# Keys laid out in SBUF as the queries are, and one transfer for each tile of four heads

## Chip, cores and metric

The kernel runs on one core of a Trainium2 chip. The metric is the device time of one execution in microseconds; the median of three runs of the kernel before is 1680.61. An interval or a verdict, where one stands, is against runs of that kernel on the same chip.

## What is computed

Packed attention, and on its output two feed-forward layers, the second gated. There are 8 batches of 8 heads, 576 tokens of 64 numbers each; 32 packing queries `p` per head stand between. All inputs and outputs are in HBM, the weights as float64, everything else as float32.

```
def sm_attn(qq, kk, vv):
    s = scale * np.matmul(qq, kk.transpose(0, 1, 3, 2))
    s = s - np.max(s, axis=-1, keepdims=True)
    a = np.exp(s)
    a = a / (np.sum(a, axis=-1, keepdims=True) + 1e-09)
    return np.matmul(a, vv)
p_packed = sm_attn(p, k, v)
out = sm_attn(q, p_packed, p_packed)
...
h = x @ w_in;  g = h * (1.0 / (1.0 + np.exp(-1.702 * h)));  x = g @ w_out
...
out = (silu(x @ w_gate) * (x @ w_val)) @ w_out2
```

The first softmax runs over the 576 keys of a head, so the order of the keys may be any, if the probabilities meet the values `v` in the same order. The values lie in chunks of 128 neighbouring tokens on the partitions.

## The kernel before, in words

PE computes in a form of three passes: each float32 operand is split into a rounded part and a rest (`split`, L205: a copy on ACT, a subtraction on DVE or POOL), and `mm3` (L215) multiplies three pairs of the parts.

Attention goes batch by batch, and in a batch by two groups `g` of four heads (HG = 4), whose 4 x 32 rows fill the 128 partitions. A batch has four raw tiles of 128 x 18 x 64 (576 KB): keys of group 0 and 1 (`load_raw` with j = 0, 1, L260) and queries of group 0 and 1 (j = 2, 3, L263). There are 8 x 4 = 32 such tiles; each comes by four DMAs on SP's queue, one per head. Of a key tile, partition i of a head holds tokens 64n + 2i and 64n + 2i + 1 for n from 0 to 8, so that the runs in HBM are 512 B. Of a query tile, partition i holds the tokens 18i to 18i + 17, one run of 4608 B. The raw tiles have three buffers, which in the first batch weights and a split query share.

`do_T` (L347) transposes a raw tile in 32 x 32 blocks on DVE, once for each half of the 64 numbers; `split_T` (L355) splits the result; `sc1` (L358) multiplies the packing queries with 320 and then 256 columns of keys into PSUM; `max1` (L367) takes the maximum; `exp1` (L375) writes the exponentials with ACT into SBUF, and on this way puts the keys into their natural order; `norm1`, `a1T`, `copy_a1T`, `pv` divide by the sum, transpose on PE, and multiply with the values. `do_D`, `sc2`, `max2`, `exp2`, `norm2` are the second attention, and `do_z` folds its packed values into the first layer's weights, so that `p1` (L554) and `p2` (L574) compute the first layer directly from the second attention's probabilities.

In the first batch the weights come too: `stage` (L294) loads float64 tiles of 512 KB, `rebias` and `to_f32` (L188, L193) turn them into float32 on ACT and DVE, `split_w` (L490) splits w_in and stores the parts to HBM with DMAs that ACT issues (L497); `split_out` does it for w_out. Later batches load the split w_in back (`load_win`, L284). While PE has nothing else, `warm` (L241) gives it matmuls without use.

The order around the change is written out by hand: FIRST (L19) is the list of steps of the first batch and of the beginning of the second, SECOND and STEADY go beside the units of the first layer. The language's planner takes the instructions in this order as priorities and places each on its engine by its own estimates of durations, so that an engine's order can differ from the list. It also gives the DMAs of SP and ACT one of eight completion semaphores in turn, and has a DMA wait until the DMA that had its semaphore before has landed. Each engine and each queue executes in order.

The first layer ends at about 855 us. From then on the second layer works without attention.

Of the kernel before, what the change touches and what calls it, by code (L numbers as in the profile page):

```python
# [11 lines left out]
AF = mybir.ActivationFunctionType  # L12
# [97 lines left out]
def kernel(  # L110
# [27 lines left out]
    PE, ACT, DVE, POOL, SP = nc.tensor, nc.scalar, nc.vector, nc.gpsimd, nc.sync  # L138
# [7 lines left out]
    G = H * NPK // P  # L146
    HG = H // G
# [5 lines left out]
    NBLK = S // 32  # L153
    NSC = 5
    TAIL = S - 4 * P
    HK = (5 * HS // 9 * 2, S - 5 * HS // 9 * 2)
# [95 lines left out]
    def load_raw(i):  # L252
        b, j = divmod(i, 2 * G)
        if b >= B:
            return
        src, g = (k, j) if j < G else (q, j - G)
        t = at.tile([P, NBLK, D], F32, tag="raw", bufs=3, name="raw")
        for h in range(HG):
            if j < G:
                SP.dma_start(out=t[32 * h:32 * h + 32].rearrange("p (n r) d -> p n (r d)", r=2),  # L260
                             in_=src[b, g * HG + h].rearrange("(n i r) d -> i n (r d)", i=32, r=2))
            else:
                SP.dma_start(out=t[32 * h:32 * h + 32].rearrange("p n d -> p (n d)"),  # L263
                             in_=src[b, g * HG + h].rearrange("(i n) d -> i (n d)", i=32))
        raw[i] = t

    def load_v(b, g):
# [59 lines left out]
    def attention(b):  # L327
        st = {}
# [46 lines left out]
        def exp1(g):  # L375
            a = at.tile([P, S], F32, tag="a1", bufs=2, name="a1")
            s = at.tile([P, 4], F32, tag="sm1", bufs=2, name="sm1")
            for t in range(2):
                o = a[:, t * HK[0]:t * HK[0] + HK[t]].rearrange("p (n i r) -> p n r i", i=32, r=2)
                ACT.activation(o, st["sc1", g][t][:, :HK[t]].rearrange("p (n r i) -> p n r i", i=32, r=2), AF.Exp,  # L380
                               bias=st["mx1", g][:, 3:4], scale=SCALE, accum_out=s[:, t:t + 1])
            st["e1", g], st["sm1", g] = a, s

# [139 lines left out]
        def raw_ahead(n):  # L523
            load_raw(b * 2 * G + n + 3)
# [338 lines left out]
    def issue(text, ops, ops_next=None):  # L863
        for x in text.split(";"):
            f, *a = x.split()
            f = ops_next[f[1:]] if f[0] == "+" else ops[f]
            f(*[int(c) if c.isdigit() else engines.get(c, c) for c in a])

    ops = dict(attention(0), load_p=load_p, load_raw=load_raw, load_v=load_v, make_consts=make_consts, stage=stage,
               rebias=lambda *k: rebias(k), to_f32=lambda kind, j, eng=ACT: to_f32((kind, j), eng), split_out=split_out, p1=u_p1, act1=u_act1,  # L870
               warm=warm,               act2=lambda n, eng=DVE: act2(units[n], eng), p2=lambda n: p2(units[n]))
    second = attention(1)
    issue(FIRST, ops, second)
    for n in range(16 + LAG, len(units)):
        b, u = units[n][0], n % NU
# [16 lines left out]
        if b == B - 1:  # L892
# [5 lines left out]
            if u in (2, 3, 21, 22, 25, 26, 29, 30):  # L898
                j = (2, 3, 21, 22, 25, 26, 29, 30).index(u)
# [79 lines left out]
```

## Time and profile before

| | us |
|---|---|
| median of three runs | 1680.61 (1678.06 to 1680.67) |
| the profiled execution | 1680.02 |
| its span, first to last instruction | 1678.3 |
| PE busy in it | 1643.6 (98%) |
| DVE, ACT, POOL busy | 1145.3, 782.1, 287.7 |
| mean granted clock of PE | 0.996 of full speed |

A row of the timeline gives the start, the busy time, engine and line, the operation with its output and inputs, how many instructions it merges, and in brackets how long the engine stood before it and what ended that. SPq and ACTq are the queues of SP and ACT that issue DMAs. `win` are the split weights in HBM, `wh` their tiles in SBUF, `w64in` and `w64out` the float64 tiles, `raw` the keys and queries, `sc` scores, `z` the folded weights, `h` and `acc` the first layer's two products. A DMA share over 1 is a few per cent of overlap in the count of busy engines.

### The profile page before, as it was taken

What the parts mean: (1) busy time and instruction counts of PE and PEld (TensorE: products, weight loads), DVE (VectorE), ACT (ScalarE), POOL (GpSimd) and SP (SyncE); (2) the same over time, 40 slices, a digit from 0 to 9 for tenths busy, and PEclk for the clock granted to TensorE, in tenths of its full rate; (3) what the DMA queues carried; (4) which work ended last, traced back from release to release, by engine and by line L of the source; (5) the groups of instructions that cost most, each with busy time, mean ns of one, the idle gap of its engine ahead of it and who ended that gap; (6) DMA issues with size and microseconds to landing.
All of it is one profiled execution on the core that took longest, in us unless ns stands there. A gap on an engine that the chain in (4) does not pass through costs nothing.

```text
span 1678.3 us, 26277 instructions
## 1 busy us (share of the span) xinstructions
PE 1643.6 (98%) x9516; PEld 1472.7 (88%) x9516; DVE 1145.3 (68%) x2161; ACT 782.1 (47%) x1662; POOL 287.7 (17%) x240
## 2 busy tenths in 40 slices
PE   9789999999999999999999999999999999999998
PEld 8679999999999999999988888888888888888887
DVE  6877878686876868777688366666657565746562
ACT  5775756566575656656554222242224222422222
POOL 2332313131221313121122111000100010001010
PEclk9999999999999999999999999999999999999999
DMA  8965767557474755526488544435444444425411
GB/s 237 341 234 130 219 187 220 175 174 229 128 232 137 220 169 173 184 90 215 152 296 317 178 162 158 145 113 168 158 145 151 130 159 145 158 75 176 145 51 51
DMA packets 169346, 290.63 MB, mean 173 GB/s; under 512 B 54784, under 2 KB 96768, under 8 KB 169216
## 3 DMA queue, kind: packets, MB, share of 16 engines
q1 hardware_dynamic: 165760, 280.03, 52.2%
q10 hardware_dynamic: 3456, 8.91, 1.4%
q8 instruction: 75, 1.23, 0.3%
q14 instruction: 55, 0.45, 0.1%
HBM read 230.16 MB, written 58.72 MB: 172 GB/s over the span
## 4 chain that ended last, share of the span: by engine, by line
PE 83%; DVE 6%; DMA 4%; issue 3%; ACT 2%; POOL 1%; SPq 0%; ACTq 0%; POOLq 0%; DVEq 0%
PE acc L217 36%; PE gv L217 30%; PE h L217 10%; PE sc L217 3%; PE pv L412 2%; PE zp L516 2%; DMA win<-wh 2%; DVE z L519 1%; DMA wh<-win 1%; DVE gh L207 1%; DVE g L566 1%; PE a1T L395 1%; DVE T L347 0%; POOL gh L207 0%; DMA w64in<-in_moe_w_in_dram 0%
## 5 line engine op out<-in xcount | busy, mean ns | idle before, releaser
L217 PE MATMUL gv<-xh,w 128*128 128x512 f32 x2304 | 554.4, 389 | 0.0
L217 PEld LDWEIGHTS gv<-xh,w 128*128 128x128 f32 x2304 | 432.4, 188 | 89.7
L217 PE MATMUL acc<-gh,wo 128*128 128x288 f32 x3072 | 457.1, 296 | 4.6 <-ACT wo L206 2.7
L217 PEld LDWEIGHTS acc<-gh,wo 128*128 128x128 f32 x3072 | 426.8, 189 | 9.0 <-ACT wo L206 3.5
L217 PE MATMUL acc<-wo,gh 128*128 128x512 f32 x1296 | 326.8, 389 | 0.4
L217 PEld LDWEIGHTS acc<-wo,gh 128*128 128x128 f32 x1296 | 243.0, 188 | 52.0 <-DVE c L211 1.6
L217 PE MATMUL h<-a,z 128*128 128x288 f32 x1536 | 251.7, 298 | 8.6 <-DVE g L566 6.8
L207 DVE TENSOR_TENSOR gh<-g,gh 128x288 fp32r<-128x288 f32 (+1 forms) x295 | 175.8, 596 | 92.7 <-ACT gh L206 89.8
L217 PEld LDWEIGHTS h<-a,z 128*128 128x128 f32 x1536 | 222.0, 189 | 16.8 <-DVE g L566 7.9
L206 ACT CAST gh<-g 128x288 fp32r<-128x288 f32 (+1 forms) x304 | 140.1, 462 | 156.1 <-DVE g L566 108.0
L207 POOL TENSOR_TENSOR gh<-s,gh 128x512 fp32r<-128x512 f32 x60 | 82.8, 1380 | 699.5 <-ACT gh L206 655.7
L810 DVE TENSOR_TENSOR c<-gv,c 128x512 f32<-128x512 f32 x192 | 132.2, 688 | 84.2 <-ACT tb L825 56.7
L206 ACT CAST gh<-s 128x512 fp32r<-128x512 f32 x60 | 37.2, 621 | 247.0 <-DVE s L821 229.2
L566 DVE SCALAR_TENSOR_TENSOR g<-sig,h 128x288 f32<-128x288 f32 x256 | 113.9, 445 | 41.9 <-ACT sig L564 37.9
L564 ACT ACTIVATE sig<-h 128x288 f32<-128x288 f32 x256 | 104.3, 408 | 76.4 <-PE h L217 73.4
L810 DVE TENSOR_TENSOR ta<-gv,c 128x512 f32<-128x512 f32 x96 | 66.2, 689 | 83.4 <-PE gv L217 83.4
L521 POOL TENSOR_TENSOR z<-z,z 128x512 fp32r<-128x512 f32 x56 | 74.9, 1338 | 175.7 <-ACT z L520 175.7
L519 DVE TENSOR_TENSOR z<-zp,z 64x512 f32<-64x512 f32 x112 | 76.5, 683 | 15.2 <-ACT z L518 12.3
L830 ACT ACTIVATE s<-c 128x512 f32<-128x512 f32 x48 | 30.3, 632 | 96.0 <-DVE c L810 96.0
L518 ACT COPY z<-zp 64x512 f32<-64x512 f32 x112 | 65.1, 581 | 13.0 <-PE zp L516 10.8
L516 PE MATMUL zp<-wh,E 128*128 128x512 f32 x224 | 66.6, 400 | 4.6 <-DMA wh<-win 2.7
L814 ACT ACTIVATE s<-ta 128x512 f32<-128x512 f32 x48 | 30.3, 632 | 69.1 <-DVE ta L810 69.1
(134 smaller groups left out, 1574.9 us busy)
## 6 DMA issues: line engine op xcount, KB each, us to landing
w<-w2s SPq DMA_DIRECT2D x144, 512.0 KB, 3.3
wh<-win SPq DMA_DIRECT2D x112, 512.0 KB, 4.2
w2s<-w SPq DMA_DIRECT2D x36, 512.0 KB, 3.8
w<-w2s SPq DMA_DIRECT2D x48, 256.0 KB, 2.6
raw<-in_k_dram SPq DMA_DIRECT2D x64, 144.0 KB, 4.4
raw<-in_q_dram SPq DMA_DIRECT2D x64, 144.0 KB, 3.3
x2d<-x SPq DMA_DIRECT2D x16, 576.0 KB, 3.3
w2d<-f SPq DMA_DIRECT2D x36, 256.0 KB, 3.1
```

The lines of the kernel that those rows point to most:

```text
L206: ACT.copy(dst[:, 0], src)
L207: eng.tensor_tensor(out=dst[:, 1], in0=src, in1=dst[:, 0].bitcast(F32), op=ALU.subtract)
L217: PE.matmul(o, lhsT=lhs(a), rhs=rhs(c), start=first and n == 0, stop=last and n == 2)
L412: PE.matmul(ps[:, c].rearrange("p h i -> p (h i)"), lhsT=vv[:n, k, 2 * c:2 * c + 2].rearrange("p h d -> p (h d)"), rhs=st["a1T", g][:n, k, ...
L516: PE.matmul(ps, lhsT=E[:, c].rearrange("p a i -> p (a i)"), rhs=w[c][:, d], start=d == 0, stop=d == 1)
L518: ACT.copy(x[o], ps[r])
L519: DVE.tensor_tensor(out=x[o], in0=ps[o], in1=x[o], op=ALU.add)
L521: POOL.tensor_tensor(out=y[:, 1], in0=x, in1=y[:, 0].bitcast(F32), op=ALU.subtract)
L564: ACT.activation(s, ps[:, :HS], AF.Tanh, scale=0.5 * 1.702)
L566: DVE.scalar_tensor_tensor(out=g, in0=s, scalar=1.0, in1=ps[:, :HS], op0=ALU.add, op1=ALU.mult)
L810: DVE.tensor_tensor(out=o, in0=ps, in1=c, op=ALU.add)
L814: ACT.activation(s1, ta, AF.Tanh, scale=0.5)
```

## The change

The branch for keys in `load_raw` goes: keys are laid out as queries are, tokens 18i to 18i + 17 on partition i of a head. The loop over the four heads goes too: one DMA brings 128 partitions of 4608 B, which are one piece of 576 KB in HBM. The column (n, i) of a score block is now the token 18i + n, so `exp1` writes 10 and then 8 blocks of 32 with a step of 18 elements in its output, where it wrote with a step of 2. Sizes and number of all other instructions stay as they are.

```
 def load_raw(i):
...
     t = at.tile([P, NBLK, D], F32, tag="raw", bufs=3, name="raw")
-    for h in range(HG):
-        if j < G:
-            SP.dma_start(out=t[32 * h:32 * h + 32].rearrange("p (n r) d -> p n (r d)", r=2),
-                         in_=src[b, g * HG + h].rearrange("(n i r) d -> i n (r d)", i=32, r=2))
-        else:
-            SP.dma_start(out=t[32 * h:32 * h + 32].rearrange("p n d -> p (n d)"),
-                         in_=src[b, g * HG + h].rearrange("(i n) d -> i (n d)", i=32))
+    SP.dma_start(out=t.rearrange("p n d -> p (n d)"),
+                 in_=src[b, g * HG:g * HG + HG].rearrange("h (i n) d -> (h i) (n d)", i=32))
...
 def exp1(g):
...
     for t in range(2):
-        o = a[:, t * HK[0]:t * HK[0] + HK[t]].rearrange("p (n i r) -> p n r i", i=32, r=2)
-        ACT.activation(o, st["sc1", g][t][:, :HK[t]].rearrange("p (n r i) -> p n r i", i=32, r=2), AF.Exp,
+        o = a.rearrange("p (i n) -> p n i", n=NBLK)[:, t * HK[0] // 32:(t * HK[0] + HK[t]) // 32]
+        ACT.activation(o, st["sc1", g][t][:, :HK[t]].rearrange("p (n i) -> p n i", i=32), AF.Exp,
                        bias=st["mx1", g][:, 3:4], scale=SCALE, accum_out=s[:, t:t + 1])
```

## Rows read from the trace of the kernel before

**Rows 1.** Windows: length, busy PE, PEld, DVE, ACT, POOL (x count), PE clock, DMA share, GB/s.

```profile
0.00:35.00 35.00, 31.43 (x232) 29.38 (x232) 22.16 (x57) 15.90 (x33) 7.69 (x15) 1.00 0.81 216
35.00:110.00 75.00, 57.88 (x342) 49.51 (x342) 59.26 (x105) 57.01 (x119) 23.47 (x21) 0.93 0.94 319
110.00:200.00 90.00, 86.67 (x614) 82.74 (x613) 72.26 (x158) 60.41 (x142) 32.15 (x27) 1.00 0.58 170
200.00:855.00 655.00, 650.10 (x4730) 635.27 (x4729) 492.70 (x1077) 403.70 (x954) 141.57 (x118) 1.00 0.58 181
```

**Rows 2.** Waits of PE from 200 to 855 us: total, times, longest.

```profile
PE zp L516 <- DMA wh<-win: 2.3, 5, 0.6
```

**Rows 3.** Windows of shorter stretches, same columns.

```profile
3.00:5.00 2.00, 2.00 (x11) 2.00 (x11) 1.00 (x2) 0.62 (x1) 0.20 (x1) 1.00 1.03 242
20.00:35.00 15.00, 14.72 (x116) 13.50 (x115) 11.08 (x30) 6.72 (x17) 3.31 (x3) 1.00 0.70 205
40.00:50.00 10.00, 8.22 (x43) 6.27 (x44) 9.54 (x19) 7.27 (x14) 2.05 (x2) 1.00 1.02 392
100.00:105.00 5.00, 4.03 (x19) 4.03 (x20) 4.19 (x8) 4.13 (x8) 2.04 (x2) 0.66 0.67 158
```

**Rows 4.** Timeline of SP's queue to 32 us: start, length of the issues, line.

```profile
1.31 1.95 SPq L260 DMA_DIRECT2D raw<-in_k_dram  x4
...
5.77 0.93 SPq L298 DMA_DIRECT2D w64in<-in_moe_w_in_dram  x2
9.78 2.19 SPq L263 DMA_DIRECT2D raw<-in_q_dram  x4
...
18.93 0.63 SPq L298 DMA_DIRECT2D w64in<-in_moe_w_in_dram  x1
27.13 2.84 SPq L274 DMA_DIRECT2D vt<-in_v_dram  x5
```

**Rows 5.** Waits of SP's queue, up to 110 us: total, times, longest.

```profile
SPq L274 <- DMA win<-wh: 10.8, 3, 7.6
```

**Rows 6.** Tile raw, DMAs issued from 1.2 to 3.2 us.

```profile
DMA to landing us min/median/max: 2.7/2.9/3.2
```

**Rows 7.** Timeline of DVE and ACT, 6 to 12 us.

```profile
6.14 1.44 DVE L347 STREAM_TRANSPOSE T<-raw 128x576 f32<-128x576 f32 x2 [2.08 <-DMA raw<-in_k_dram]
...
9.79 0.66 ACT L190 ACTIVATE f<-w64in 128x512 f32<-128x512 f32 x1 [1.50 <-DMA w64in<-in_moe_w_in_dram]
```

**Rows 8.** Timelines of SP, ACT, DVE, PE near 95 us, and tile raw there.

```profile
91.89 6.25 SPq L260 DMA_DIRECT2D raw<-in_k_dram  x8
...
96.95 0.59 ACT L206 CAST z<-zp 128x512 fp32r<-128x512 f32 x1 [2.32 <-DMA raw<-in_k_dram]
...
98.61 0.78 DVE L347 STREAM_TRANSPOSE T<-raw 128x576 f32<-128x576 f32 x1 [3.75 <-DMA raw<-in_k_dram]
...
100.97 1.44 PE L217 MATMUL h<-a,z 128*128 128x288 f32 x6 [4.76 <-DVE g L566]
...
DMA to landing us min/median/max: 2.9/4.7/5.1
```

**Rows 9.** Groups of ACT by shape: count, busy us, mean ns, idle before.

```profile
L206 ACT CAST gh<-g 128x288 fp32r<-128x288 f32 x256 | 110.4, 432 | 109.2 <-DVE g L566 108.0
...
L206 ACT CAST gh<-g 128x512 fp32r<-128x512 f32 x48 | 29.7, 620 | 46.8 <-PE acc L217 46.8
...
L380 ACT ACTIVATE a<-sc,mx 128x320 f32<-128x320 f32 x16 | 8.8, 549 | 5.5 <-DVE mx L372 5.5
...
L380 ACT ACTIVATE a<-sc,mx 128x256 f32<-128x256 f32 x16 | 7.8, 486 | 0.0
```

**Rows 10.** Chain of the first 110 us: shares by line; start, length.

```profile
by line: DMA win<-wh 27.8%; DMA w64in<-in_moe_w_in_dram 5.9%; issue 5.6%; DMA raw<-in_q_dram 5.1%; PE pv L412 4.3%; DMA raw<-in_k_dram 4.2%; PE sc L217 3.4%; DVE wh L207 3.0%; POOL wo L207 2.9%; DVE T L347 2.5%; POOL wh L207 2.5%; DMA pt<-i
...
82.04 9.76 DMA win<-wh
```

**Rows 11.** Timeline of ACT's queue near 24 us.

```profile
24.04 0.93 ACTq L497 DMA_DIRECT2D win<-wh  x2
```

## The prediction

> **What bounds the kernel now.** I read the page's first part, then the span by stages, then PE's waits in the long middle stage, and at last the start of the kernel engine by engine. By the page PE is busy nearly all the time; the stages say where it isn't [rows 1]: in the first 110 us PE lacks 3.6 + 17.1 = 20.7 us, and some of what it does there is only the filler of `warm`; from 110 to 200 us it lacks 3.3, and in the 655 us after that 4.9. From 855 us on the kernel has no attention in it, so the change can't reach that. In the middle the change can save at most those 3.3 + 4.9 us, and the largest wait of PE in the second of them is 2.3 us for weights that come back from HBM [rows 2], not a key, a query or a softmax. So the change is decided in the first 110 us, where DMA is the fullest resource (0.81, then 0.94 of its time) and PE the one with holes.
>
> Two things are to be seen in that start. First, what a key costs. While key tile 0 alone is in flight, 3 to 5 us, the DMA engines are full (1.03) and move 242 GB/s; with 4 KB rows, 40 to 50 us, as full (1.02) they move 392 [rows 3]. Second, the queue. SP issues the 13th DMA at 9.78 us though the 12th was out at 6.70, and after 19.56 it issues nothing until 27.13 [rows 4]; it stood there for the landing of a weight store, 7.6 us [rows 5]. The program gives its DMAs eight completion semaphores in turn, those of SP and ACT together, and a DMA is not issued before the one eight places back has landed. Four small DMAs per tile eat four of the eight places.
>
> **The change, part by part.** 128 DMAs of keys and queries become 32. An issue takes 0.45 us (four in 1.95) [rows 4], so some 43 us of SP's time go, over 700 us, nearly all beside other work. Terms, with gains negative:
>
> (a) The first key. The four DMAs go out at 1.31 to 2.8, and land 2.7 to 3.2 us after each issue [rows 6], the last at 6.0; DVE waits for it 2.08 us until 6.14 [rows 7]. One DMA issued at 1.31 has its first quarter in at 1.31 + 2.7 = 4.0; the other 0.44 MB take 1.1 us at 392 GB/s or 1.8 at 242, so it lands at 5.1 or 5.8. I take 392, since its rows of 4608 B are nearest to the 4 KB rows: 0.9 us earlier. Behind it the first weight tile goes out at 1.8 and not at 3.29, and ACT's 1.50 us of waiting for it until 9.79 [rows 7] can go, with what DVE then waits for ACT. Bounds -0.2 to -2.2; I take -1.5, because the chain from the transpose to the maximum is mostly work that stays.
>
> (b) The hole in SP's queue. DMA runs at 0.70 of its time from 20 to 35 us [rows 3]: 0.30 x 15 = 4.5 us of transfer are lost, just ahead of a stretch in which DMA is full (1.02 from 40 to 50 us). Nine fewer DMAs stand ahead of the hole, so the queue gets further before a store stops it. But the two stores themselves go out at 24.04 [rows 11], when the weights have been split, and that work stays, and some DMA will still stand eight places behind them. Bounds 0 to -4.5; I take -1.0, near the end where the stop only changes places.
>
> (c) Key tile 0 of the second batch. Its four DMAs go out at 91.89, when a store has landed and given its buffer free; they take 4.7 us in the median to land, DVE stands 3.75 us for them until 98.61, ACT 2.32 us until 96.95, and PE 4.76 us until 100.97 [rows 8], and after that rest the granted clock of 100 to 105 us is 0.66 [rows 3], part of them at the lower level of 1.2 GHz: 0.34 x 5 = 1.7 us more. ACT doesn't read keys: its next store has the semaphore of the first of the four, and all of ACT queues behind that store. With one DMA per tile the store eight places back is another DMA, and the tile, by the reckoning of (a), lands at 91.89 + 2.7 + 1.1 = 95.7 and not near 98.5. Weight stores share the engines at that time (one has just landed, 82.04 + 9.76 = 91.80 [rows 10]), so this can shrink to nothing. The buffer isn't free earlier. Bounds 0 to -(2.8 + 1.7) = -4.5; I take -2.5: ACT's 2.3 and a little of the clock.
>
> (d) The exponential. Its output now steps by 72 bytes and not by 8. Two instructions per group take 549 + 486 ns; contiguous casts of 288 and 512 elements take 432 and 620 [rows 9], 0.84 ns an element, so the same sizes written contiguously would take 459 + 405. The excess is 0.17 us, accumulation included; no row has the wider step. Bounds 0 to 0.84 x 576 = +0.48 us a group (an element taking twice its time). Two groups lie on the path of the start; the others hide in ACT, which is busy 403.7 of 655 us from 200 us on [rows 1]. If that cover went, all 16 would cost at most 7.7 us. I take +0.1 a group, +0.2, near the excess that the row has, and bounds 0 to +1.0. The Trainium skill, SBUF — State Buffer, Door 1: The DMA port swizzle, speaks against this part: accesses that leave a 16-byte line each pay, and four float32 are as far as a step is free. The rows agree so far that a step of 8 bytes is not free; by the rule this term would go to its upper end, +1.0, and the sum to -4.0.
>
> (e) Transposes, splits, scores, the values and the outputs keep their sizes: the columns of a score block are other keys, and the exponential puts them back in order. Keys and queries of batches 2 to 7: 0, hidden under PE's own work; the tile is waited for as a whole by one transpose before and after.
>
> **Sum:** -1.5 - 1.0 - 2.5 + 0.2 = -4.8 us. The profiled execution took 1680.02 (span 1678.3 and 1.7 around it), 0.6 below the median of 1680.61. So 1675.2 by the one and 1675.8 by the other; I say 1675.5.
>
> **Rivals.**
> *Absorbed.* 27.8% of the chain of the first 110 us are stores of split weights, the last of them 9.76 us long [rows 10]; they hold the buffers of the next weights. If they set the pace up to 92 us, what (a) and (b) gain is waited off there, and of (c) the next late thing takes over: ACT and DVE are busy 57.0 and 59.3 of the 75 us from 35 on [rows 1], with weights that DMA alone doesn't finish. Then 1679 to 1681. For it: the stores' share of the chain. Against it: DVE's and ACT's stops at 94 us lie behind the last store.
>
> *A bulk load in a store's way.* With fewer small DMAs in the round of eight, the DMA eight places back from a store is oftener a load of 512 KB or a whole tile that was issued a few us before. ACT, with exponentials, sigmoids and splits behind the store, then stands until it lands. The price is in the trace: a stop of 2.32 us of ACT goes with 4.76 us of PE and 1.7 of clock, 6.5 together. One such stop at 40 to 90 us, where a DMA needs up to 9.8 us to land [rows 10], undoes the gain and leaves +2 to +6: 1683 to 1687. It decides as soon as that load lands over 2 us later than the store is ready. For it: (c) is such a stop. Also, the order of each engine's instructions is the planner's and moves with its estimate of every DMA, so that none of these places is certain. Against it: each round of eight then also holds more bytes, and SP reaches later loads sooner.
>
> *No faster per byte.* Key runs are 512 B now. If the slow rate at 3 to 5 us belongs to the start and not to the runs, a tile takes 2.4 us as before: (a) shrinks to -0.2 and (c) to ACT's semaphore, some -2 in all, 1678 to 1679. Against it: 242 beside 392 GB/s at equally full engines. The Trainium skill, DMA: Bandwidth & Descriptors, Specifications, has 512 B as the least run for line rate, which is this rival; the two rates in the trace don't bear it out.
>
> **How the numbers follow.** A measurement here tells 0.2%, some 3.4 us. Forecast (faster, 1668 to 1677): 0.56. Absorbed 0.16 and no faster per byte 0.06, both within 0.2%: 0.22. The bulk load: 0.22, slower. The best ends of (a) to (c) are -2.2 - 4.5 - 4.5 = -11.2, 1669; the rival's middle is 1685. The range 1668.5 to 1685 leaves out the tails; the forecast's own is 1669 to 1677.
>
> **What would show it.** Right: the first transposes start at 5.2 and not 6.14; the key tile of (c) lands in 4 us or less where the median of the small ones was 4.7; SP's hole is shorter; ACT's store near 96 us no longer ends with a key's landing, and PE's 4.76 us before 101 shrink by over 2; the second layer begins 4 to 5 us earlier, and from there on nothing else moves. (d): 549 and 486 ns grow by under 100. Wrong: the second layer begins no earlier, or PE has a new hole between 20 and 110 us that ends with ACT, and ACT's with a load's landing; or the transposes start early and the first scores don't; or PE lacks more than 4.9 us between 200 and 855.

## The result, and the profile after

The changed kernel takes 1700.17 us (1699.18 to 1701.02, 4 runs) beside 1679.99 for the kernel before on the same chip: a ratio of 1.0123, 95% interval 1.0111 to 1.0135. It is 20 us slower. The profiled execution took 1699.18 us, its span is 1697.5.

The windows of the kernel after, with the stages and columns of [rows 1]:

```profile
0.00:35.00 35.00, 29.47 (x213) 27.99 (x214) 24.36 (x60) 19.66 (x39) 7.97 (x15) 0.95 0.94 310
35.00:110.00 75.00, 61.17 (x351) 52.27 (x349) 55.12 (x99) 51.76 (x110) 22.23 (x20) 0.89 0.82 289
110.00:200.00 90.00, 85.75 (x599) 81.03 (x600) 73.42 (x155) 60.46 (x140) 31.64 (x28) 1.00 0.51 164
200.00:300.00 100.00, 96.97 (x695) 93.47 (x694) 76.48 (x166) 62.80 (x148) 24.02 (x20) 1.00 0.58 190
300.00:600.00 300.00, 291.48 (x2086) 283.84 (x2085) 220.54 (x485) 182.33 (x427) 68.70 (x57) 0.99 0.53 176
600.00:855.00 255.00, 253.49 (x1856) 248.60 (x1855) 185.39 (x402) 152.12 (x359) 46.88 (x40) 1.00 0.48 162
```

DMA did what was hoped of it: in the first 35 us it moves 310 GB/s where it moved 216. PE did not follow. From 200 to 855 us it now lacks 3.0 + 8.5 + 1.5 = 13.0 us where it lacked 4.9. In the first of these stages DMA, too, is less busy than before, 0.58 of its time against 0.69; the kernel before there:

```profile
200.00:300.00 100.00, 99.64 (x727) 97.33 (x726) 76.80 (x170) 63.85 (x153) 24.79 (x21) 1.00 0.69 207
```

The stores of the first layer's output, two for each batch, give the course of the loss: the first of them starts 3.1 us later than in the kernel before (136 us), the ones at 248, 400, 502 and 602 us are 5.1, 11.8, 16.7 and 19.0 us late, and the last, with which the second layer begins, 19.2 us. After that nothing is lost. The store at 602 us, first after, then before:

```profile
602.35 0.38 SPq L582 DMA_DIRECT2D x2d<-x  x1
583.36 0.38 SPq L587 DMA_DIRECT2D x2d<-x  x1
```

So most of the loss lies where the prediction put nothing, in batches 2 to 7.

The waits of PE there (total, times, longest), as in [rows 2]:

```profile
PE zp L511 <- DMA wh<-win: 8.7, 8, 2.9
PE zp L511 <- ACT sig L559: 1.7, 1, 1.7
PE zp L511 <- DVE z L514: 0.9, 1, 0.9
```

The wait for w_in's split parts on their way back was 2.3 us and is 8.7. These loads were not changed; they stand in SP's queue beside the tiles. The timeline of SP's queue from 359 us on, first after (L258 the tiles, L284 the weights):

```profile
359.29 0.80 SPq L284 DMA_DIRECT2D wh<-win  x2
364.56 0.33 SPq L258 DMA_DIRECT2D raw<-in_k_dram  x1
365.01 0.83 SPq L284 DMA_DIRECT2D wh<-win  x2
373.12 0.33 SPq L258 DMA_DIRECT2D raw<-in_k_dram  x1
373.54 16.56 SPq L284 DMA_DIRECT2D wh<-win  x7
```

and the same place of the work before (L260 the keys, L289 the weights):

```profile
357.38 0.86 SPq L289 DMA_DIRECT2D wh<-win  x2
358.29 0.92 SPq L260 DMA_DIRECT2D raw<-in_k_dram  x2
363.10 1.13 SPq L289 DMA_DIRECT2D wh<-win  x2
364.27 0.43 SPq L260 DMA_DIRECT2D raw<-in_k_dram  x1
368.83 1.71 SPq L289 DMA_DIRECT2D wh<-win  x2
370.60 0.42 SPq L260 DMA_DIRECT2D raw<-in_k_dram  x1
374.56 0.79 SPq L289 DMA_DIRECT2D wh<-win  x2
375.41 0.42 SPq L260 DMA_DIRECT2D raw<-in_k_dram  x1
377.87 0.32 SPq L289 DMA_DIRECT2D wh<-win  x1
```

A batch loads thirteen weight tiles in this stretch and keys of the next batch between them. Written as a row (w a weight, 0 and 1 DMAs of the next batch's first and second key tile):

```
before  w w w w 0 w w 0 0 w w 0 w w 1 w w 1 w ... 1 1
after   w w w w 0 w w 1 w w w w w w w
```

Before, the quarters of a tile are spread between the weights, and the first quarter of tile 1, the one that must wait for a free buffer, comes behind ten of the thirteen weights. After, the whole tile 1 is one DMA, and the planner puts it behind six. It can't go out before its buffer is free: VectorE's transposes of this batch's second key tile read that buffer, the last of them from 372.33 to 373.09 us, and the DMA goes out at 373.12. From 365.84 to then SP issues nothing, and seven weights queue behind. A weight, too, has to wait for a buffer, which PE's products of the folding (`zp`) set free. But those at 370.07 us were over at 371.16, and both next weights go out at once behind the tile, at 373.54 and 374.02: it was the tile's DMA that held them, for over 2 us. Here is PE's timeline at that place, and under it two pieces of the chain that ended last in it:

```profile
370.07 1.09 PE L511 MATMUL zp<-wh,E 128*128 128x512 f32 x4
...
379.89 0.70 PE L511 MATMUL zp<-wh,E 128*128 128x512 f32 x2 [2.54 <-DMA wh<-win]
```

```profile
374.02 5.74 DMA wh<-win
...
386.48 3.51 DMA wh<-win
```

PE stands 2.54 us until the second of these weights has landed (374.02 + 5.74 = 379.76), and the granted clock of 380 to 400 us is 0.91, part of it at the lower level of 1.2 GHz, where it was 1.00 before. In the 40 us from 360 PE has 249 matmuls; before it had 282. All of SP's waits at a tile's DMA from 126 to 880 us, after:

```profile
SPq L258 <- DVE g L561: 40.0, 9, 4.7
SPq L258 <- DVE gh L207: 36.1, 6, 7.5
SPq L258 <- DVE sm L381: 14.9, 4, 4.0
SPq L258 <- DVE T L342: 8.1, 3, 3.4
```

That is 99.1 us. Before, the same waits make 21.8: these two, 1.6 for `gh` and 1.3 for others.

```profile
SPq L260 <- DVE g L566: 14.2, 3, 4.7
SPq L263 <- DVE g L566: 4.7, 1, 4.7
```

What SP waits for is VectorE's progress up to a transpose; the profile names the VectorE instruction that ended last.

### The profile page after: what moved, and what is told of

It reads as the page before. It is cut to its first block, busy times and chain, and to the rows that moved or that the text cites. A ratio compares the mean times of both kernels' runs of the same rounds, so it can differ in the third digit from the quotient of the medians.

```text
span 1697.5 us, 26144 instructions
## 1 busy us (share of the span) xinstructions
PE 1652.9 (97%) x9516; PEld 1479.4 (87%) x9516; DVE 1151.8 (68%) x2161; ACT 786.9 (46%) x1662; POOL 288.6 (17%) x240
## 4 chain that ended last, share of the span: by engine, by line
PE 77%; DVE 7%; issue 6%; DMA 5%; ACT 2%; POOL 2%; ACTq 0%; SPq 0%; POOLq 0%; DVEq 0%
PE acc L217 32%; PE gv L217 29%; PE h L217 8%; PE pv L407 2%; PE sc L217 2%; PE zp L511 2%; DMA wh<-win 2%; DVE gh L207 1%; DVE z L514 1%; DVE g L561 1%; DVE T L342 1%; POOL wo L207 1%; POOL gh L207 0%; DVE f L202 0%; PE a1T L390 0%
```

## The experiments

Two theories stood at the outset: **Q**, SP's queue as just read, and **E**, the exponential with its wider step. Later a third came in, **P**: the planner, which sees one DMA for a tile, also moves transposes on VectorE.

**One part at a time.** e1 is the kernel before with the new order of the tokens in the exponential's output alone; e2 is the changed kernel with the old step. In both the probabilities meet the values in another order, with the same sizes, so that neither computes this attention.

```
e1:  loads of before;  exp1 writes with a step of 18
e2:  one DMA per tile; exp1 writes with a step of 2
```

> The kernel before, with only the exponential of the first softmax written with a step of 18 elements (loads as before; the probabilities then meet the values in another order, same sizes). Every engine has the instruction order of the kernel before. Theory Q (SP's queue: one transfer per tile changes the planned order, and weight loads stand behind a raw tile's wait for its buffer): 1679 to 1683 us, no more than the two exponentials of the start, 2 x 0.56 = 1.1 us. Theory E (the exponential: 858 + 734 ns where there were 549 + 486, 16 groups, delays the chain of attention, and the weight loads and folds come late with it): 1690 to 1700. Both needed together: 1682 to 1690.

> The changed kernel, with the exponential written with the old step of 2 elements (the probabilities then meet the values in another order, same sizes). Every engine has the instruction order of the changed kernel. Theory Q: 1697 to 1701 us, PE's wait for wh<-win at 8 us as in the changed kernel. Theory E: 1676 to 1682, that wait near 2.7. Both needed together: 1685 to 1695.

e1: 1681.52 beside 1680.03, ratio 1.0006 [0.9996, 1.0015]. e2: 1694.65, 1.0087 [1.0065, 1.0110]. The step alone costs nothing that can be measured, and the loads alone carry most of the loss, so E falls. But e2 missed Q's 1697 to 1701 and lies, at its upper end, in the range given for both needed together. Its runs lie from 1691.6 to 1699.8, so that nothing is read from the 5 us between e2 and the full change: whether the step adds to the loads' loss stays open.

**Layout or number of DMAs, keys or queries.** e3 keeps layout and step of the change, but brings each tile by four DMAs. e4 is the kernel before with one DMA for a query tile, e6 the changed kernel with four for a query tile.

```
e3:  for h in range(HG):
         SP.dma_start(out=t[32 * h:32 * h + 32]..., in_=src[b, g * HG + h].rearrange("(i n) d -> i (n d)", i=32))
e4:  keys as before (4 DMAs, 512 B runs); queries: 1 DMA
e6:  keys: 1 DMA; queries: 4 DMAs, the rest as in the change
```

> The changed kernel's layout and its step of 18 in the exponential, but four transfers per tile, one per head, as before. Theory Q: 1678 to 1685 us, since the queue has as many transfers as before and the tiles can go out in quarters between the weight loads. Theory E: 1695 to 1701. If what matters is any new order of the planner, it can be anywhere in 1680 to 1700, and the waits of SP at the raw loads tell.

> The kernel before, with only the query tiles by one transfer (keys as before, four transfers, step 2). Theory Q: slower than before if it is the whole-tile transfer that stands in the way of weight loads, by up to half of the 20 us (1682 to 1692), unless the key tiles alone do it (1678 to 1682). Theory E: 1676 to 1681, no exponential is changed.

> The changed kernel with the query tiles by four transfers again; key tiles by one. The program puts the second key tile behind the sixth weight load, as in the changed kernel. Theory Q with the key tile as the cause: 1694 to 1702 us. If it takes keys and queries together (fewer places in the round of eight): 1682 to 1690.

e3: 1679.47 beside 1680.03, 0.9996 [0.9987, 1.0005]: runs of 4608 B and the wider step together neither gain nor lose. e4: 1682.68, 1.0015 [1.0005, 1.0024], +2.6 us. e6: 1702.93 beside 1679.89, 1.0137 [1.0120, 1.0153], +23 us. So it is the number of DMAs, and of the key tiles above all; and as e3 has the new layout with the old number of DMAs, it isn't the layout. PE's waits for weights from 200 to 855 us go with it: 10.1 us in e2, 9.6 in e6, 8.7 in the full change, and none in e1, e3 and e4.

**The place of the second key tile.** e5 is the changed kernel; only the DMA of the next batch's second key tile is fixed in SP's order behind the tenth weight: `raw_tile_ahead` takes the buffer at the old place, `raw_last` issues the DMA and keeps it in program order.

```
-    11: "... pv 0; raw_ahead 2",
+    11: "... pv 0; raw_tile_ahead 2",
-    26: "do_z 3; split_a2 0 1; win 12; split_a2 0 0",
+    26: "do_z 3; split_a2 0 1; win 12; raw_last 2; split_a2 0 0",
```

> The changed kernel, with one thing moved from the third batch's attention on: the buffer of the second key tile is taken where it was, but its one transfer is issued behind the tenth of the thirteen weight loads of a half batch (it stood behind the sixth). Theory Q: SP no longer stands for that tile's buffer ahead of seven weight loads; PE's wait for wh<-win after 110 us falls from 8.7 to 4 us or less, and the time from 1700 to 1681 to 1690. If the size of the transfer, and not its place, is what delays the loads: 1695 to 1701. Theory E, already weakened, has nothing to gain here: 1698 to 1701.

1684.41 beside 1679.89, 1.0031 [1.0019, 1.0042]: 16 of the 20 us are back with one DMA of each batch moved. (PE's waits for weights after 110 us fell to 5.4 and not to 4 or less, in a trace of the longest of its six runs.) SP's waits at tiles are down from 99.1 us to these:

```profile
SPq L267 <- DVE T L352: 8.1, 3, 3.4
SPq L267 <- DVE gh L207: 6.4, 2, 4.3
```

**Early and late batches.** e7 uses one DMA for the first eight tiles and four after them, e8 the reverse; e10 uses one for the first batch's four tiles only, e11 for the second batch's four only.

```
e7:   if i < 8:        one DMA    else: four
e8:   if i < 8:        four       else: one DMA
e10:  if i < 4:        one DMA    else: four
e11:  if 4 <= i < 8:   one DMA    else: four
```

> The changed kernel with one transfer per tile only for the tiles of the first two batches, and four for the later ones. Theory Q: what the first 130 us lose stays (3 us) and the growth from 200 to 600 us goes: 1681 to 1686. If the growth is set off by a start that is out of step: 1693 to 1701.

> The other way round: four transfers for the tiles of the first two batches, one for the later ones. Theory Q: the growth alone, 1693 to 1699. If the growth needs the start: 1679 to 1684.

> One transfer a tile for the first batch's four tiles only (tiles 0 to 3, up to 25 us), four transfers for all others. The first two batches by one transfer cost 5 us. If that arises at the start (the tiles are sooner out of SP's queue but the fourth tile's transfer competes with weights, and PE starves near 75 us): first h at +1.4 to +3, second layer at +3 to +5, 1682 to 1685. If it arises where the second batch's keys stand near 90 us: 1679.5 to 1681.5.

> The counterpart: one transfer a tile for the second batch's four tiles only (tiles 4 to 7, issued from 90 to 150 us), four for all others. If the loss of the first two batches arises at the start: 1679.5 to 1681.5, first h as before. If it arises at the second batch's keys and queries: 1682 to 1685, with the loss between 95 and 250 us. Both theories have the two runs add up to about +5.

| | us | before | ratio, interval |
|---|---|---|---|
| e7, tiles 0 to 7 | 1684.87 | 1679.89 | 1.0026 [1.0016, 1.0037] |
| e8, tiles 8 to 31 | 1697.41 | 1679.89 | 1.0101 [1.0085, 1.0116] |
| e10, tiles 0 to 3 | 1680.14 | 1680.28 | 0.9998 [0.9989, 1.0008] |
| e11, tiles 4 to 7 | 1688.89 | 1680.28 | 1.0050 [1.0036, 1.0064] |

e7 and e8 add up to 22.5, near the 20 of the whole. e10 and e11 do not add up to e7, though both theories expected it: the second batch alone loses 8.6, more than with the first and beyond the 1682 to 1685 named for it. e11's trace shows a second place. VectorE and PE in e11 near 95 us:

```profile
98.47 0.78 DVE L347 STREAM_TRANSPOSE T<-raw 128x576 f32<-128x576 f32 x1 [8.07 <-DMA raw<-in_k_dram]
99.17 0.65 DVE L202 SCALAR_TENSOR_TENSOR f<-f,wc 128x512 int32<-128x512 int32 x1
...
100.53 0.80 PE L217 MATMUL zp<-wh,F 128*128 128x512 f32 x1 [6.25 <-ACT wh L206]
```

The tile goes out no earlier than before (92.41 and 91.89 [rows 8]) and lands in 6.0 us. But the transpose that reads it stands seven instructions further ahead in VectorE's order, before the instruction that puts a float32 weight together (`f`, L202) and six more. Before, these ran first and VectorE stood 3.75 us for the tile [rows 8]; now it stands 8.07 with them behind it, ACT stands 6.91 for `f`, and PE 6.25 for ACT.

**The order of VectorE.** e12 is e11 with that one transpose kept where the written list has it.

```
             d = DVE.transpose(out=t, in_=raw[i]...)
+            if i == 4 and e == 0:
+                tc.keep_in_program_order(d)
```

> One transfer a tile for the second batch's four tiles only, as in e11, but the first transpose of the second batch's first key tile is kept at its place in the written list, behind the split and sigmoid work that it had been moved ahead of; the transfers are unchanged. Theory P (the planner, by its estimate of one transfer, puts the waiting transpose ahead of other work of VectorE, and VectorE stands for the tile with that work behind it): PE's 6.3 us of waiting for ACT's wh near 100 us go, and the time falls from 1688.9 to 1680 to 1683. Rival (the whole tile lands late, 6.0 us after its issue, and whatever waits for it is late): 1686 to 1689, with the stop somewhere else.

1681.60 beside 1679.27, 1.0013 [1.0004, 1.0023]: 6.3 of 8.6 us are back, and VectorE has no wait for a tile left from 85 us on, though the slowest of the three DMAs issued from 92.7 to 99.7 lands in 7.0 us. So P holds for e11, and the landing time isn't what decides.

**Repairs together.** e9 has e5's place and four DMAs for the first two batches; e13 is e9 with four for all queries. e14 is e5 with the transpose of e12 and those of the later second key tiles kept in the list's order. e15 has all tiles by one DMA, the second key tile's behind all thirteen weights, and e12's transpose.

```
e15  26: "do_z 3; split_a2 0 1; win 12; split_a2 0 0",
     31: "do_z 6; win 15; raw_last 2; do_z 7",     and e12's three lines
```

> The changed kernel with both causes that the runs so far point to taken away: the eight tiles of the first two batches come by four transfers each, as before, and from batch 2 on one transfer a tile, the second key tile's issued behind the tenth of the thirteen weight loads. Theory Q (SP executes in order; a tile's single transfer, placed ahead of weight loads while its buffer is still awaited, holds them): of the 20 us, 16 go with the place of the second key tile and 3 to 5 with the first two batches, so 1679 to 1682, ratio 0.9995 to 1.001, the second layer begins within 2 us of before, and PE's waits for weights from 200 us on are under 3 us. Rival (the two repairs act on the same microseconds, since either lets the attention run ahead): 1683 to 1685, the time with the place alone mended. That it beats the kernel before by over 0.2% (under 1677) is expected by neither: from 200 to 855 us the kernel before has under 5 us to give.

> As e9 (the first two batches by four transfers a tile, the second key tile of later batches by one transfer behind the tenth weight load), and the queries of all batches by four transfers again; only the keys of batches 2 to 7 come by one. Queries alone by one transfer cost 2.6 us (e4). If what e9 still loses between 200 and 500 us belongs to the query tiles: 1681 to 1684, and the second layer begins 2 to 3 us earlier than in e9. If it belongs to the keys, above all to the late place that the repair gives the second key tile: 1685.5 to 1687, as e9.

> The changed kernel, all tiles by one transfer, the second key tile's transfer of each steady batch behind the tenth weight load (as e5), and the first transpose of the second batch's first key tile and of the second key tile of each later batch kept at their place in the written list. Theory P (the waiting transposes are put too early on VectorE): the 4.4 us that e5 still loses go, 1679 to 1682, the second layer begins within 2 us of before. Rival (the place of the transfer is what is left, or the transfers themselves): 1683 to 1686, as e5.

> The changed kernel, all tiles by one transfer, the second key tile's transfer of each steady batch behind all thirteen weight loads, and of the transposes only the second batch's first kept in its written place. If what e5 loses is weight loads that still stand behind the key tile's transfer: 1679 to 1682. If it is VectorE at a transpose that waits for that tile: it is no better than e5, 1683 to 1687, since the tile comes later still.

| | us | before | ratio, interval |
|---|---|---|---|
| e9 | 1686.25 | 1680.28 | 1.0038 [1.0025, 1.0050] |
| e13 | 1687.24 | 1679.27 | 1.0053 [1.0036, 1.0070] |
| e14 | 1684.06 | 1679.68 | 1.0026 [1.0016, 1.0036] |
| e15 | 1680.11 | 1679.68 | 1.0004 [0.9994, 1.0013] |

e9 missed theory Q's 1679 to 1682, and with 1686.25 its rival's 1683 to 1685 as well; the rival was nearer. e13 says that the rest isn't the queries'. e14 missed theory P's 1679 to 1682: as a whole its kept transposes gain nothing over e5. Its PE waits for weights only 0.2 us from 200 to 855, and it still loses 4:

```profile
PE zp L523 <- DMA wh<-win: 0.2, 1, 0.2
```

The stores of the first layer's output in its trace are 2.8 us late at 196 us, 4.7 at 295 and 4.0 at the last, so what is left arises before 300 us. e15 has neither loss; from 130 us on its stores are never more than 1.3 us late. SP's queue in e15, at the place of the timelines above:

```profile
344.77 33.82 SPq L294 DMA_DIRECT2D wh<-win  x13
378.63 0.42 SPq L267 DMA_DIRECT2D raw<-in_k_dram  x1
```

and its window from 200 to 855 us, as the last of [rows 1]:

```profile
200.00:855.00 655.00, 650.33 (x4734) 635.77 (x4733) 505.46 (x1078) 406.69 (x956) 138.48 (x118) 1.00 0.53 180
```

PE's 650.33 is the 650.10 of before. So one DMA per tile, with 4608 B rows and the wider step, costs nothing that can be measured once the second key tile's DMA and one transpose are kept in a good order, and gains nothing either. No version beat the kernel before by more than its interval. Two ends stay open. Why the place behind ten weights loses 4 us that the place behind thirteen does not, with hardly a wait for weights left, isn't settled; e14 and e15 differ in the kept transposes too. And how much of the full change's 20 us is P's isn't shown, since e15's two repairs were not run one by one: in e5 the transpose near 95 us stands as early as in e11, but waits 1.48 us and not 8.07, and the store at 194 us is only 0.8 late. A fourth buffer for the tiles, which could take SP's wait away without touching the order, wasn't tried.

## Why the prediction was wrong

**(e), the step that failed.** It costed keys and queries of batches 2 to 7 at nothing, "hidden under PE's own work", because the tile is waited for as a whole before and after. That looks only at who waits for the tile. What waits behind the tile's DMA was left out: weights, in a queue that executes in order, behind a DMA that has to wait for a buffer. The cover, PE's other work, is gone as soon as such a weight comes 2.5 us late. Taken alone, these batches cost 17.5 us (e8), and 16 of the 20 go with the place of one DMA a batch (e5). The prediction had named the sign by which it would be wrong: PE lacking more than 4.9 us between 200 and 855. It lacks 13.0.

**(a) The first key.** The first transposes start at 5.81 us, 0.33 earlier, not 0.9:

```profile
5.81 1.44 DVE L342 STREAM_TRANSPOSE T<-raw 128x576 f32<-128x576 f32 x2 [2.11 <-DMA raw<-in_k_dram]
```

The tile lands 4.5 us after its issue, the later of the two bounds and not the rate taken: 392 GB/s was too much for it. The transposes start early and the first `h` (46.9 us) is 1.4 us late.

**(b) The hole in SP's queue.** The one stop of 7.6 us is gone, but SP's waits for stores up to 35 us are 8.4 us in three stops, where they were 7.9: the stop changed places, as the prediction feared. More loads are out ahead of it, and DMA moves 337 GB/s from 5 to 35 us where it moved 229. What was to come of it did not: VectorE has a transpose of the last query tile, moved ahead here too, and stands for it with the copy behind it that PE's next product needs. VectorE and PE of the kernel after:

```profile
25.29 0.78 DVE L342 STREAM_TRANSPOSE T<-raw 128x576 f32<-128x576 f32 x1 [1.73 <-DMA raw<-in_q_dram]
...
27.03 2.54 PE L407 MATMUL pv<-a1T,vt 128*128 128x64 f32 x16 [2.33 <-DVE a1T L397]
```

PE is busy 2.97 of the 5 us from 25 on, and the granted clock of 30 to 35 us is 0.74. By e10 the first batch comes out at nothing: what DMA gains is lost there, or was never on the path. The rival "absorbed" had the right outcome for this stage alone.

**(c) The second batch's first key.** The tile takes 5.0 us from 89.91 and not under 4. As foreseen ACT no longer stands for a key, but its 2.32 us of [rows 8] turn into two other waits of 2.4, for `f` and for `zp`, and PE stands near 97 and 103 us:

```profile
89.91 5.00 DMA raw<-in_k_dram
```

```profile
94.93 0.78 DVE L342 STREAM_TRANSPOSE T<-raw 128x576 f32<-128x576 f32 x1 [3.58 <-DMA raw<-in_k_dram]
```

```profile
96.98 0.50 PE L217 MATMUL zp<-wh,F 128*128 128x512 f32 x1 [1.75 <-ACT wh L206]
...
103.69 1.33 PE L217 MATMUL h<-a,z 128*128 128x288 f32 x6 [2.36 <-DVE g L561]
```

PE's 4.76 us of [rows 8] are 1.75 and 2.36 now, and the transpose stands ahead of the same seven instructions of VectorE as in e11, `f` the first of them. What (c) meant does exist where the order is kept: in e12 the store at 131 us is 1.6 us earlier than before. It is given back by 243 us.

**(d) The exponential.** The sign was right, the size not. The groups by shape, as in [rows 9]:

```profile
L375 ACT ACTIVATE a<-sc,mx 128x320 f32<-128x320 f32 x16 | 13.7, 858 | 3.6 <-DVE mx L367 3.4
L375 ACT ACTIVATE a<-sc,mx 128x256 f32<-128x256 f32 x16 | 11.7, 734 | 0.0
L375 ACT ACTIVATION_READ_ACCUMULATOR a<-sc,mx 128x1 f32 x32 | 7.2, 224 | 0.0
```

The accumulator's read of before, which [rows 9] leave out:

```profile
L380 ACT ACTIVATION_READ_ACCUMULATOR a<-sc,mx 128x1 f32 x32 | 6.1, 190 | 0.0
```

858 + 734 against 549 + 486 are 0.56 us a group, and the two reads of the accumulator add 0.07; taken were 0.1, with an upper bound of 0.48. It was costed off the path, and there it stayed (e1). The Trainium skill, SBUF — State Buffer, Door 1: The DMA port swizzle, has accesses that leave a 16-byte line pay each, and the trace agrees in direction: 0.97 ns more an element at 72 bytes than at 8.

**The rivals.** "A bulk load in a store's way" had the right kind, an engine that stands with good work behind a transfer, and the wrong place: it looked for ACT behind a store in the first 110 us and priced one stop. The stops are SP's behind a buffer, once a batch, and VectorE's at 95 us. Its sentence that the order of each engine's instructions "moves with its estimate of every DMA" stood there as an uncertainty, and was the cause. "No faster per byte" came near for the first tile, 0.33 us earlier where it had 0.2; for the stage the 337 beside 229 GB/s of (b) speak against it. Neither decided the time.

## What to carry to other kernels

Where a planner sets the order, a change in the number of DMAs can change the order of every engine that waits for them: compare the two instruction orders before pricing anything. For each DMA or instruction that has to wait, ask what is queued behind it on its own engine, not only who waits for its result. A transfer that waits for a buffer goes behind the urgent loads of its queue; cut in four, it did that here by accident.

## What the runs showed that was not expected

Faster transfers at the start were worth nothing: with the first batch by one DMA a tile (e10) DMA moves 307 GB/s in the first 35 us, where it moved 216, and the end moves by 0.1 us. The Trainium skill, SBUF — State Buffer, The DMA setup-cost knee, fits a load by some 2 us and its bytes over 436 GB/s, an estimate of 3.4 us for a tile of 590 KB, and advises to make loads as large as can be. The trace agrees on the load, 3.2 us at the least and 4.0 in the median of 32; following the advice as it stands cost 20 us here. The median of the quarter tiles before is 4.0 us as well: beside other traffic, a load of four times the bytes landed, in the median, no later after its issue.

Writing an activation's result with a step of 72 bytes costs 0.97 ns an element more than with 8. That is over the 0.84 ns, a doubling, which the prediction held for the most, and in this kernel it cost nothing that could be measured (e1).
